# Attention and a gated long convolution on one core: from 2 by 384 to a 3 by 256 transform with woven products

## The chip, the core and the metric

The kernel runs on one core of a Trainium2 chip. A core has TensorE (PE in the profile), which multiplies matrices into PSUM; VectorE (DVE), ScalarE (ACT) and GpSimd (POOL), which work element by element; and SyncE (SP), which here only issues DMAs. The metric is device time in microseconds. Three runs of the kernel before took 190.65, 190.84 and 192.29 us; the median is 190.84.

## The reference

An attention over 4 batches, 8 heads, 768 positions and 64 channels per head. Heads with a flag see all earlier positions; the others see the first 4 positions and a window of the last 64. Its output, laid out as 4 x 768 x 512, goes through a gated convolution over the whole sequence:

```python
a = np.exp(scores - scores.max(-1, keepdims=True))      # scores masked per head
x = (a / a.sum(-1, keepdims=True)) @ v                  # 4 x 8 x 768 x 64, then to 4 x 768 x 512
proj = x @ w_proj
x1, x2, x3 = proj[..., :D], proj[..., D:2*D], proj[..., 2*D:]
X2 = np.fft.rfft(x2, n=S, axis=1)
H = np.fft.rfft(filter_fft, n=S, axis=0)
x2_conv = np.fft.irfft(X2 * H, n=S, axis=1)
out = (x1 * x2_conv * x3) @ w_out
```

D is 512 and S is 768. The transform is linear along the sequence, so it can be applied to x ahead of the product with the middle part of w_proj.

## The kernel before

The work is cut into named steps. The strings AHEAD and FAST list all steps in the order in which they are issued, with the PSUM bank they write (behind @) and the engine of those that can go to more than one (/v VectorE, /s ScalarE, /p GpSimd). Nothing is reordered later: each engine runs its steps in that order and waits on semaphores for what other engines make. A second, general kernel stands behind a branch for other flags; it isn't run here.

Heads are handled in 16 pairs, n = 0 to 15, four pairs to a batch b. Per pair: lk, lq, lv load k, q and v (SP issues them, L1369 and L1383); ck, cq, cv cast them; T and E bring q and k into the layout with channels on partitions, by TensorE and a copy for the first eight pairs, by a DMA transpose after that; sc are the products of scores (L1452), ex their exponentials on ScalarE (L1471); the mask is applied either by products that add a large negative bias (sb, L1465, for n below BIASED_FAST) or by multiplying the exponentials (mk and mr, L978); at are the products with v (L1516), rec and nm the normalization (L1533). A pair is all-causal (RR), all-windowed (LL) or mixed (RL); every four pairs have the same kinds in the same order.

Forward transform of a pair: fd and fe fold the two halves of the sequence into a difference and a sum of 384 rows; fA, fS, fb and fr combine their three blocks of 128; the half-transforms W (L1569, L1571, L1573; two per pair, each of three products of 256, 256 and 128 columns) give the spectrum of one chain in one PSUM bank each, written word after word; We evicts both. tn and te turn the normalized output (by TensorE for the pairs in TURNED_BACK, else by DMA) into xT.

Per batch b: X (L1620) multiplies the spectrum with the middle part of w_proj, in three tiles of two halves, four products of 512 columns each; Xe evicts; pa, pb, pc multiply with the filter's spectrum HAB (complex, on VectorE); sw are two DMAs that exchange the halves of a tile for pb. For each block cb of 128 channels: x1 and x3 (L1655) are the outer two projections; xs evicts x1; g multiplies x1 and x3. The inverse transform c (L1685) has two sums of three products of 384 columns, each sum in a bank of its own; ce copies one of them to SBUF as f_evs, and cv (L1696) adds and subtracts the other, which gives the two halves of the sequence; y multiplies with the gate. o (L1712) is the product with w_out, oe evicts, st stores.

Once at the start: iota, sine and cosine make the tables G of the forward transform; Gt (L1227) turns them on TensorE into the tables Gi of the inverse one. The filter is loaded by GpSimd's queue (lfilt, L1236), as are the weights (lw, lwo); F (L1265) transforms it with 18 products, H scales it into HAB, and Hd are two DMAs that exchange halves. blank (L1041) are 29 products of zeros, five in AHEAD and twelve pairs in FAST.

Of the kernel before, what the change touches and what calls it, by code (L numbers as in the profile page):

```python
# [9 lines left out]
FP32 = mybir.dt.float32  # L10
# [103 lines left out]
SIXTHS = (0, 1, 2, 3, 4, 5, 6, 7, 8, 9, 10, 11, 12, 13, 14, 15)  # L114
# [7 lines left out]
lflag lk0 lq0 lk1 lq1 mblank want tcol fcol0 table sin0 fcol1 blank0@6 tfrac quarter mtab0 par turns other angle  # L122
ident mtab1 wrap size sin cos
# [3 lines left out]
ones1 ones2 mtab3 blank5@0 lq2 lk2 blank10@1 ck0/v skew0/s lv0 parb skew1/p G32/s T0.1@2 xp0 cq0/v lk3 blank6@3  # L127
mtab2 E0.1/v lv1 blank8@4 Gk1/s lv3 blank7@5 Gm00 btab G31/p blank1@6 ck1/v kz1 lq3 T0.0@7 lk4 alt blank3@0 Gm2
cq1/s G30/p Gh0 lq4 T1.1@1 Gm01 kz0 lv2 E0.0/s G00/v T1.0@3 G01/p Gm1 cq2/s lk6 E1.1/v sc0.1@4 sb0.1 lq6 ck2/p
sc0.3@6 ex0.1 Gh1 E1.0/v sc0.4@0 ones0 kx1/p sb0.4 lk5 sb0.3 T2.1@2 ex0.4 kz2 lk7 sc0.0@4 E2.1/v lq5 cv0/p sb0.0  # L130
Gt1@3 ex0.3 lq7 blank2@0 kx2/v Gt2@1 Gk0/p ex0.0 lv6 T2.0@2 ks1/p Ge2/v ck3/p sc0.2@6 Ge1/s E2.0/v sc1.2@4 sb1.2
lfilt sb0.2 T3.1@0 ex1.2 sc0.5@2 Gt0@1 ex0.2 cv1/v sc2.3@4 E3.1/v lv4 vx1/p sb0.5 ex0.5 sc1.0@6 lw2.1 Ge0/v
sb1.0 ks2/s vs1/v at0.0@2 lw2.0 ex1.0 at0.1 cq3/v lw0.1 T3.0@0 ex2.3 kx3/v sc1.1@6 rec0 lw1.1 sb1.1 nm0/v cv3/s
blank11@1 ex1.1 sc2.1@4 fe0/p sb2.1 tn0@1 cq4/v E3.0/s at1.0@2 lw0.0 blank9@6 ex2.1 ks3/v sc2.4@6 ck4/v at1.1
lw1.0 ex2.4 T4.0@0 T4.1@4 vs3/v E4.0/s te0/v lwo sc3.1@6 sb3.1 rec1 E4.1/s nm1/v fd0/p sc3.2@0 sb3.2 ex3.1 fe1/v
tn1@5 fS0/p ex3.2 sc3.0@2 fold0/v sb3.0 sc2.0@6 ex3.0 vx3/v fd1/v F0.0@4 fA0/v fA1/p F0.1@0 H0.0/s fS1/v fb0/p
sb2.0 fold1/v sc2.2@2 H0.1/s sb2.2 ex2.0 fb1/p te1/v F1.0@1 fr1 ex2.2 F2.1@4 fr0 cv2/v H1.0/s F2.0 lv5 vs2/v
vx2/p H0.2/v at2.0@6 H2.0/s at2.1 ck6/p sc4.0@2 H2.1/s rec2 Hd0 at3.0@0 nm2/v at3.1 H2.2/s lk9 rec3 fe2/p F1.1@6
# [790 lines left out]
def patterned(tc, pools, pre, q, k, v, flags, n_sink, window, moe_w_proj, moe_filter_fft, moe_w_out, out):  # L929
# [912 lines left out]
```

## Time and profile before

| | |
|---|---|
| median of three runs | 190.84 us |
| profiled execution | 190.27 us |
| its span, first to last instruction | 188.4 us |
| granted TensorE clock, mean | 0.985 |
| DMA queue 1 (issued by SP): packets, MB, share of 16 engines | 75986, 30.81, 73.9% |
| DMA queue 0 (issued by GpSimd): packets, MB, share | 2944, 2.88, 9.1% |

Busy time is the time in which an engine had at least one instruction under way. Products overlap in TensorE's pipeline, so the mean duration of one is longer than its share of the time; the distance between the starts of neighbours, or a piece of the chain of waits divided by its count, is what one costs in a stream. The chain of waits follows the work that ended last back through whatever released each step. In rows of groups, the second number behind the bar is the mean duration of one instruction in ns, and what stands behind the second bar is idle time of the engine just ahead of it.

### The profile page before, as it was taken

What the parts mean: (1) busy time and instruction counts of PE and PEld (TensorE: products, weight loads), DVE (VectorE), ACT (ScalarE), POOL (GpSimd) and SP (SyncE); (2) the same over time, 40 slices, a digit from 0 to 9 for tenths busy, and PEclk for the clock granted to TensorE, in tenths of its full rate; (3) what the DMA queues carried; (4) which work ended last, traced back from release to release, by engine and by line L of the source; (5) the groups of instructions that cost most, each with busy time, mean ns of one, the idle gap of its engine ahead of it and who ended that gap; (6) DMA issues with size and microseconds to landing.
All of it is one profiled execution on the core that took longest, in us unless ns stands there. A gap on an engine that the chain in (4) does not pass through costs nothing.

```text
span 188.4 us, 4493 instructions
## 1 busy us (share of the span) xinstructions
PE 176.5 (94%) x1694; PEld 103.4 (55%) x1694; DVE 161.2 (86%) x329; ACT 145.6 (77%) x210; POOL 69.0 (37%) x103
## 2 busy tenths in 40 slices
PE   7879999989998999999999999999999999999970
PEld 2437664647745563575555656655657765555530
DVE  6887799789889999999989999999899996499810
ACT  5787899999999999988989999696977332426360
POOL 5874785554322224670250460700650630000000
PEclk9978999999999999999999999999999999999997
DMA  4999999999999999999999989982162002312074
GB/s 152 330 274 279 208 197 236 270 286 251 213 202 225 215 185 166 233 219 213 202 233 228 228 221 238 250 87 56 60 98 111 3 2 111 135 36 111 11 286 157
DMA packets 78955, 34.01 MB, mean 180 GB/s; under 512 B 68306, under 2 KB 75218, under 8 KB 78930
## 3 DMA queue, kind: packets, MB, share of 16 engines
q1 hardware_dynamic: 75986, 30.81, 73.9%
q0 software_dynamic: 2944, 2.88, 9.1%
q8 instruction: 14, 0.23, 0.5%
q14 instruction: 11, 0.09, 0.2%
HBM read 24.64 MB, written 6.29 MB: 164 GB/s over the span
## 4 chain that ended last, share of the span: by engine, by line
PE 66%; ACT 14%; DVE 6%; DMA 5%; issue 3%; POOL 2%; SPq 2%; DVEq 0%; ACTq 0%; POOLq 0%
PE space L1655 18%; PE space L1712 11%; PE space L1620 8%; PE space L1452 7%; PE space L1685 7%; PE space L1516 6%; ACT f_pT L1471 4%; DMA f_qkT<-f_qk_bf 3%; ACT f_HAB L1274 3%; DMA f_v_f<-in_v_dram 2%; PE space L1465 2%; ACT f_qk_bf L975 2%; SPq L1383 2%; PE space L1569 1%; PE space L1571 1%
## 5 line engine op out<-in xcount | busy, mean ns | idle before, releaser
L1471 ACT ACTIVATE f_pT<-space 128x1024 bf16<-128x1024 f32 (+3 forms) x68 | 58.8, 917 | 6.1 <-PE space L1465 1.9
L1655 PE MATMUL space<-f_xT,f_wproj 128*128 128x384 bf16 x256 | 47.9, 326 | 0.1
L1655 PEld LDWEIGHTS <-f_wproj 128*128 128x128 bf16 x256 | 24.0, 98 | 17.1 <-issue 1.0
L1712 PE MATMUL space<-f_wout,r_gy 128*128 128x512 bf16 x96 | 24.7, 379 | 0.0
L1452 PE MATMUL space<-f_qkT 64*128 64x128 bf16 (+3 forms) x248 | 22.6, 253 | 1.1 <-DVE f_attn L1533 0.5
L1620 PE MATMUL space<-f_wproj,f_xh 128*128 128x512 bf16 x96 | 22.7, 379 | 0.1
L1685 PE MATMUL space<-f_Gi,r_P 128*128 128x384 bf16 x96 | 19.0, 326 | 0.7 <-ACT f_evs L975 0.3
L978 DVE TENSOR_TENSOR f_pT<-f_pT,r_mtab 128x1024 bf16<-128x1024 bf16 (+3 forms) x33 | 18.5, 583 | 0.8 <-ACT f_pT L1471 0.6
L975 ACT COPY f_o<-space 128x1024 f32<-128x1024 f32 (+1 forms) x12 | 9.9, 836 | 11.3 <-PE space L1712 11.2
L1516 PEld LDWEIGHTS <-f_pT 128*128 128x128 bf16 x472 | 16.7, 97 | 3.6 <-issue 0.9
L1516 PE MATMUL space<-f_v_aug,f_pT 128*128 128x65 bf16 x392 | 17.9, 193 | 0.6 <-ACT f_X L975 0.5
L1452 PEld LDWEIGHTS <-f_qkT 64*128 64x128 bf16 x248 | 10.3, 94 | 13.1 <-issue 10.4
L978 POOL TENSOR_TENSOR f_uv<-f_fo 128x256 bf16<-128x256 bf16 x12 | 9.1, 766 | 21.1 <-DVE f_fo L978 15.8
L1696 DVE TENSOR_TENSOR f_conv<-f_evs,space 128x384 bf16<-128x384 f32 x32 | 16.1, 545 | 0.6 <-PE space L1685 0.3
L975 ACT CAST f_xh<-space 128x768 bf16<-128x768 f32 x14 | 11.2, 808 | 4.9 <-PE space L1573 4.6
L1620 PEld LDWEIGHTS <-f_xh 128*128 128x128 bf16 x96 | 9.0, 98 | 10.0 <-issue 0.4
L1712 PEld LDWEIGHTS <-r_gy 128*128 128x128 bf16 x96 | 9.0, 98 | 8.9 <-issue 0.4
L1533 DVE TENSOR_TENSOR f_attn<-space,f_rec 128x768 bf16<-128x768 f32 x14 | 13.4, 955 | 0.4
L1685 PEld LDWEIGHTS <-r_P 128*128 128x128 bf16 x96 | 8.8, 97 | 7.4 <-issue 1.1
L978 POOL TENSOR_TENSOR f_fo<-f_attn 128x384 bf16<-128x384 bf16 x11 | 10.4, 960 | 2.4 <-DVE f_attn L1533 1.9
L975 ACT CAST f_X<-space 128x1024 bf16<-128x1024 f32 x8 | 8.2, 1020 | 2.8 <-PE space L1620 2.7
L978 POOL TENSOR_TENSOR f_pT<-f_pT,r_mtab 128x512 bf16<-128x512 bf16 (+1 forms) x6 | 6.8, 1146 | 9.1 <-ACT f_pT L1471 9.1
(136 smaller groups left out, 345.7 us busy)
## 6 DMA issues: line engine op xcount, KB each, us to landing
f_v_f<-in_v_dram SPq DMA_DIRECT2D x32, 192.0 KB, 4.7
out_dram<-f_o SPq DMA_DIRECT2D x9, 512.0 KB, 3.1
r_qk_f<-in_k_dram SPq DMA_DIRECT2D x10, 192.0 KB, 4.4
r_qk_f<-in_q_dram SPq DMA_DIRECT2D x10, 192.0 KB, 5.0
r_qk_f<-in_k_dram SPq DMA_DIRECT2D x4, 384.0 KB, 11.3
r_qk_f<-in_q_dram SPq DMA_DIRECT2D x4, 384.0 KB, 6.1
f_qk_f<-in_q_dram SPq DMA_DIRECT2D x4, 384.0 KB, 5.8
f_qk_f<-in_k_dram SPq DMA_DIRECT2D x4, 384.0 KB, 6.6
```

Source lines behind the costliest of these rows:

```text
L975: nc.scalar.copy(out=out, in_=in_)
L978: (nc.gpsimd if now["engine"] == "p" else nc.vector).tensor_tensor(out, a, b, op)
L1274: nc.scalar.activation(out=out_(), in_=in_(), func=AF.Copy, scale=w / S)
L1452: nc.tensor.matmul(sc[:, bank, col:col + 128 * cnt], lhsT=keys, rhs=qkT(n)[rows, 0, 128 * i:128 * (i + cnt)], start=(col == 0 or not biase ...
L1471: nc.scalar.activation(out=pT(n)[:, c, :, 0:w], in_=held[f"sc.{n}.{c}"][:, :, 0:w], func=AF.Exp, scale=SCALE)
L1516: nc.tensor.matmul(att[:, hh, 65 * i:65 * i + 65], lhsT=pT(n)[:, c, bank, col:col + 128], rhs=values, start=(z == 0), stop=(z == len(here) ...
L1533: nc.vector.tensor_mul(attn(n).rearrange("p i hh d -> p hh i d"), rows[:, :, :, 0:64], held[f"rec.{n}"][:, :, :, None].to_broadcast([128, ...
L1620: nc.tensor.matmul(ps[:, u, :], lhsT=xh(b)[:, cc, chain, 128 * part:128 * part + 128], rhs=wproj()[:, cc, DM:2 * DM], start=(cc == 0), sto ...
L1655: nc.tensor.matmul(ps[:, s, 0:HS], lhsT=wproj()[:, cc, part * DM + cb * 128:part * DM + (cb + 1) * 128], rhs=xT(b)[:, cc, s * HS:s * HS + HS],
L1685: nc.tensor.matmul(ps[:, 0, 0:HS], lhsT=P(b)[:, t, u, ch], rhs=Gi()[:, tile_no], start=(m == 0), stop=(m == 2))
L1696: fn(conv[:, half * HS:half * HS + HS], held[f"evs.{b}.{cb}"], held[f"c_ps.{b}.{cb}.1"][:, 0, 0:HS])
L1712: nc.tensor.matmul(ps, lhsT=gy(b)[:, cb, i * 128:(i + 1) * 128], rhs=wout()[:, cb, :], start=(cb == 0), stop=(cb == NC - 1))
```

## The change

The order 2 by 384 becomes the prime-factor order 3 by 256. What is computed stays the same; the steps between change, and with them the whole order string.

- The two half-transforms of a pair write into the same bank, one the even and the other the odd words, 512 words in the first bank and 256 in the second (`woven`); the eviction then reads 768 words in a row. Products and columns stay as they were.
- The filter goes the same way: folds, the same four combinations (fAF, fSF, fbF, frF), eight half-transforms K, an eviction Ke, 24 transposes F, and scalings H. The 18 products and the exchanging DMAs go.
- The tables of the inverse transform come straight from sine and cosine; the 18 transposes go.
- A three-point step of nine operations per batch (qa, qs, qr, qh, qz, qd, qb, qp, qm) stands between the spectrum's product and the inverse. The DMA exchanges sw go; pb reads X itself.
- The inverse has six products of 256 columns per block of channels, in sums of two, for the three classes of positions modulo 3. ce and the two cv per block go. In batches 0 to 2, y reads the result straight from PSUM; in batch 3, one cv on ScalarE copies 768 columns to SBUF first.
- Positions in gy are sorted by class, so g and xs read PSUM with a step of three words, and stores write rows that lie three apart.
- BIASED_FAST goes from 4 to 8: pairs 4 to 7 get bias products, and their mk and mr steps go. Pair 14 leaves TURNED_BACK. A one-element GpSimd copy, gate, that reads the loaded k of pair 3 stands ahead of lfilt.
- The order string is new throughout. In batch 3, x1 and x3 products stand between the spectrum and the inverse, and all o2 products ahead of the spectrum. The same 29 blank products remain; nine of the twelve pairs in FAST stand ahead of the first scores (seven before).

```diff
-TURNED_BACK = (0, 1, 2, 3, 4, 5, 6, 7, 14, 15)
-BIASED_FAST = 4
+TURNED_BACK = (0, 1, 2, 3, 4, 5, 6, 7, 15)
+BIASED_FAST = 8
+DIRECT = ((0, 0), (0, 1), (0, 2), (0, 3), (1, 0), (1, 1), (1, 2), (1, 3), (2, 0), (2, 1), (2, 2), (2, 3))
...
+    @op("gate")
+    def _():
+        nc.gpsimd.tensor_copy(out=buf("gate", [1, 1], FP32), in_=held["qk_f32.3"][0:1, 0, 0, 0, 0:1])
...
+    def spectrum(ps, u, uv, br, ch):
+        woven = lambda bank, count: ps[:, bank, 0:2 * count].rearrange("p (f u) -> p u f", u=2)[:, u]
+        nc.tensor.matmul(woven(0, 256), lhsT=br[:, 1, u, ch], rhs=G()[:, 3 * u:3 * u + 2], start=True, stop=False)
+        nc.tensor.matmul(woven(0, 256), lhsT=uv[:, 2 * u, ch], rhs=Gk()[:, u], start=False, stop=True)
+        nc.tensor.matmul(woven(1, 128), lhsT=br[:, 0, u, ch], rhs=G()[:, 3 * u + 2], start=True, stop=True)
+
+    def taken(x, ps):
+        ev(x.rearrange("p g f -> p (g f)"), ps.rearrange("p a f -> p (a f)")[:, 0:S])
...
-                ps = banks(f"W_ps.{n}")
-                if n in SIXTHS:
-                    nc.tensor.matmul(ps[:, u, 0:256], lhsT=br(n)[:, 1, u], rhs=G()[:, 3 * u:3 * u + 2, 0],
-                                     start=True, stop=False)
-                    nc.tensor.matmul(ps[:, u, 0:256], lhsT=uv(n)[:, 1 + 2 * u], rhs=Gk()[:, u],
-                                     start=False, stop=True)
-                    nc.tensor.matmul(ps[:, u, 256:384], lhsT=br(n)[:, 0, u], rhs=G()[:, 3 * u + 2, 0],
-                                     start=True, stop=True)
...
+                spectrum(banks(f"W_ps.{n}"), u, uv(n), br(n), slice(0, 128))
...
-            ev(xh(b)[:, hp], held[f"W_ps.{n}"][:, :, 0:HS])
+            taken(xh(b)[:, hp], held[f"W_ps.{n}"])
...
+    def classes(ps):
+        return ps[:, :, 0:HS].rearrange("p h (t s) -> p s h t", s=3)
...
+        @op(f"qa{b}")
+            two(SD(b)[:, 0:2], P(b)[:, 1], P(b)[:, 2], ALU.add)
+        @op(f"qs{b}")
+            two(SD(b)[:, 2:4], P(b)[:, 1], P(b)[:, 2], ALU.subtract)
+        @op(f"qr{b}")
+            scale(SD(b)[0:1], flat(b)[0:1, 2:6], 2.0)
+        @op(f"qh{b}")
+            scale(Y0(b), P(b)[:, 0], 0.5)
+        @op(f"qz{b}")
+            two(Y0(b), Y0(b), SD(b)[:, 0:4:3], ALU.add)
+        @op(f"qd{b}")
+            scale(SD(b)[:, 1:3], SD(b)[:, 1:3], 2.0 * KAPPA)
+        @op(f"qb{b}")
+            two(P(b)[:, 0], P(b)[:, 0], SD(b)[:, 0:4:3], ALU.subtract)
+        @op(f"qp{b}")
+            two(flat(b)[:, 2:4], P(b)[:, 0], SD(b)[:, 1:3], ALU.add)
+        @op(f"qm{b}")
+            two(flat(b)[:, 4:6], P(b)[:, 0], SD(b)[:, 1:3], ALU.subtract)
...
-            for r in range(2):
-                @op(f"c{b}.{cb}.{r}")
-                    ps = banks(f"c_ps.{b}.{cb}.{r}", count=1)
-                    for m, (t, u, tile_no) in enumerate(INVERSE[r]):
-                        nc.tensor.matmul(ps[:, 0, 0:HS], lhsT=P(b)[:, t, u, ch], rhs=Gi()[:, tile_no],
-                                         start=(m == 0), stop=(m == 2))
...
+            @op(f"c{b}.{cb}")
+                ps = banks(f"c_ps.{b}.{cb}").rearrange("p a f -> p (a f)")
+                for s, (re, im) in enumerate(POINTS):
+                    for c, rows in enumerate((re, im)):
+                        rhs = Gi()[:, c].rearrange("p a f -> p (a f)")[:, START[s]:START[s] + 256] if s else Gj()[:, c]
+                        nc.tensor.matmul(ps[:, 256 * s:256 * s + 256], lhsT=rows(b)[:, ch], rhs=rhs,
+                                         start=(c == 0), stop=(c == 1))
+
+            if (b, cb) not in DIRECT:
+                @op(f"cv{b}.{cb}")
+                    ev(buf(f"conv.{b}.{cb}", [128, S], BF16, f"conv{cb % 2}"),
+                       held[f"c_ps.{b}.{cb}"].rearrange("p a f -> p (a f)")[:, 0:S])
...
+                if (b, cb) in DIRECT:
+                    to = y if cb < NC - 1 else buf(f"conv.{b}.{cb}", [128, S], BF16, f"conv{cb % 2}")
+                    nc.vector.tensor_mul(to, held[f"c_ps.{b}.{cb}"].rearrange("p a f -> p (a f)")[:, 0:S], x)
...
+                    rows = out[b].rearrange("(n p s) c -> s p n c", p=128, s=3)[i // 2]
```

The order of batch 3 after the change, from its first spectrum product to its inverse:

```
X3.2.0@0 st2.1 X3.2.1 X3.1.0@4 Xe3.2/s X3.1.1 pb3.2/v X3.0.0@2 pa3.2/v Xe3.1/s x13.0.0@0
pc3.2/v oe2.5/s pb3.1/v X3.0.1 pa3.1/v st2.5 x13.0.1 Xe3.0/s pc3.1/v x13.3.0@4 xs3.0/s pa3.0/v x13.2.0@6 qa3/v
x13.3.1 pb3.0/v x33.0.0@2 xs3.3/s qs3/v x13.1.0@0 pc3.0/v qr3/s x33.0.1 qh3/v x13.1.1 g3.0 x33.1.1@4 qd3/s qb3/v
x33.1.0 qz3/v x13.2.1 xs3.1/s qp3/v x33.2.1@2 xs3.2/s qm3/v x33.2.0 g3.1 c3.0@0 g3.2 c3.1@6 cv3.0/s c3.2@4
```

More of the change, by code (lines that the diff above doesn't have):

```diff
@@ L1252, in _ @@
     def _():
-        two(fold()[:, 0], filt()[:, 0:NM, :], filt()[:, NM:NT, :], ALU.subtract)
+        two(fold()[:, 0], filt()[:, 0:NM, :], filt()[:, NM:NT, :], ALU.add)
     @op("fold1")
     def _():
-        two(fold()[:, 1], filt()[:, 0:NM, :], filt()[:, NM:NT, :], ALU.add)
-    for t, pieces in enumerate((((0, 0), (0, 1)), ((1, 3), (1, 4)), ((0, 2), (1, None)))):
-        for u, (chain, tile_no) in enumerate(pieces):
-            @op(f"F{t}.{u}")
-            def _(t=t, u=u, chain=chain, tile_no=tile_no):
-                ps = banks("F_ps2")[:, u] if t == 2 else banks(f"F_ps{t}.{u}", count=1)[:, 0]
-                for m in range(NM):
-                    nc.tensor.matmul(ps, lhsT=Gh()[:, m] if tile_no is None else G()[:, tile_no, m, :],
-                                     rhs=fold()[:, chain, m, :], start=(m == 0), stop=(m == NM - 1))
```

428 lines of the change are left out of this document (205 added, 223 removed).

## The prediction

> **What bounds the kernel now.** I read the busy shares first, then busy time by stage, then the chain of waits, then groups by form. The first fence is from the page: the span, the busy shares, and the chain's shares by engine. The second is busy time in five stretches (columns: stretch, its length, then busy us and instruction count of PE, weight loads, VectorE, ScalarE, GpSimd; granted clock; DMA share; GB/s).
>
> ```profile
> span 188.4 us, 4493 instructions
> PE 176.5 (94%) x1694; PEld 103.4 (55%) x1694; DVE 161.2 (86%) x329; ACT 145.6 (77%) x210; POOL 69.0 (37%) x103
> ...
> PE 66%; ACT 14%; DVE 6%; DMA 5%; issue 3%; POOL 2%; SPq 2%; DVEq 0%; ACTq 0%; POOLq 0%
> ```
>
> ```profile
> 0.00:40.00 40.00, 35.95 (x396) 20.72 (x397) 32.80 (x73) 34.17 (x46) 25.99 (x53) 0.96 1.07 245
> 40.00:80.00 40.00, 37.79 (x404) 22.94 (x403) 37.24 (x78) 39.31 (x57) 15.09 (x19) 1.00 1.10 217
> 80.00:120.00 40.00, 40.00 (x400) 23.52 (x399) 38.08 (x83) 36.16 (x54) 15.13 (x20) 1.00 1.17 227
> 120.00:160.00 40.00, 40.00 (x379) 24.67 (x378) 36.59 (x73) 25.40 (x41) 12.76 (x14) 1.00 0.37 75
> 160.00:188.40 28.40, 22.73 (x121) 11.51 (x118) 16.46 (x27) 10.60 (x15) 0.00 (x0) 0.96 0.34 122
> ```
>
> Two regimes show. Up to 80 us ScalarE is fullest (39.31 of 40 us from 40 to 80) and TensorE is idle for 4.05 + 2.21 = 6.3 us. From 80 to 160 us TensorE has no idle time at all, and VectorE is close behind with 38.08 + 36.59 = 74.7 of 80 us. So what TensorE no longer does after 80 us comes off the span, as long as VectorE can follow; before 80 us extra TensorE work is partly free. The chain of waits (start, us, what) shows the end:
>
> ```profile
> 166.29 0.65 PE space L1655 x4
> ...
> 171.11 2.44 PE space L1685 x15
> ...
> 177.55 5.19 PE space L1712 x24
> ...
> 182.77 0.59 ACT f_o L975
> ```
>
> From 166.29 to 182.74 us it is products alone, then a copy (L975) and the last store. I take the price of a product from its share of the chain or from the distance between starts, since the mean of a row holds the pipeline's depth too: 2.44/15 = 0.163 us for 384 columns (L1685), 0.65/4 = 0.163 again (L1655), 5.19/24 = 0.216 for 512 (L1712).
>
> **The inverse transform.** A block of 128 channels now takes six products of 256 columns, not six of 384. The price of 256 columns comes from the forward transform in the timeline of TensorE (start, us, line):
>
> ```profile
> 39.84 0.27 PE L1569 MATMUL space<-r_G,f_br 128*128 128x256 bf16 x1 [0.25 <-ACT f_pT L1471]
> 39.95 0.27 PE L1571 MATMUL space<-f_Gk,f_uv 128*128 128x256 bf16 x1
> 40.05 0.22 PE L1573 MATMUL space<-r_G,f_br 128*128 128x128 bf16 x1
> 40.11 0.27 PE L1569 MATMUL space<-r_G,f_br 128*128 128x256 bf16 x1
> ```
>
> Starts lie 0.11 and 0.10 apart, and a half of the transform (256, 256 and 128 columns) takes 40.11 - 39.84 = 0.27; with 0.055 for 128 columns that is 0.107 for 256. Sixteen blocks: 96 x 0.163 = 15.6 becomes 96 x 0.107 = 10.3, so -5.3 us, nearly all of it after 80 us.
>
> **Setup, filter, transposes.** Pieces of the chain price these:
>
> ```profile
> 18.09 0.44 PE space L1227 x6
> ...
> 29.66 0.77 PE space L1265 x3
> ...
> 148.10 0.33 PE space L1589 x6
> ```
>
> The 18 transposes of the inverse tables (L1227) go: about -1.3 at 0.44 per six. The filter's 18 products (L1265, 512 columns) cost 18 x 0.216 = 3.9; in their place come eight halves at 0.27 and 24 transposes at 0.055 (six take 0.33, L1589), 3.5 in all: -0.4. Pair 14 goes back by DMA, not by transposes: -0.3, after 80 us. The blank products stay 29; of their twelve pairs nine now stand ahead of the first scores, seven before. There TensorE waits for loads and table work in either order, so the move costs 0; without that cover two pairs cost 4 x 0.216 = 0.9, within the 6.3 us of idle time of that stage.
>
> **Masks of pairs 4 to 7** become bias products, as pairs 0 to 3 have them. Pairs 0 to 3 have the same kinds, so their 33 products are the price (three forms, counts behind x):
>
> ```profile
> L1465 PE MATMUL space<-f_btab,r_identity 128*128 128x512 bf16 x10 | 3.2, 384 | 0.0
> L1465 PE MATMUL space<-f_btab,r_identity 128*128 128x128 bf16 x18 | 2.7, 249 | 0.0
> L1465 PE MATMUL space<-f_btab,r_identity 128*128 128x384 bf16 x5 | 1.3, 332 | 0.0
> ```
>
> At the spacing above that is 10 x 0.216 + 5 x 0.163 + 18 x 0.057 = 4.0 us more for TensorE. Together with setup and filter it makes 4.0 - 1.3 - 0.4 = +2.3 before 80 us. There ScalarE ends most waits and TensorE has 6.3 us idle, so it costs between 0 and 2.3; I take 1.0.
>
> **VectorE.** Rows by form (line, operation, shapes, count | busy, mean ns):
>
> ```profile
> L1696 DVE TENSOR_TENSOR f_conv<-f_evs,space 128x384 bf16<-128x384 f32 x32 | 16.1, 545 | 0.6 <-PE space L1685 0.3
> L978 DVE TENSOR_TENSOR r_P<-r_P,f_m 128x1024 bf16<-128x1024 bf16 x12 | 8.2, 687 | 0.1
> L978 DVE TENSOR_TENSOR f_pT<-f_pT,r_mtab 128x1024 bf16<-128x1024 bf16 x12 | 8.1, 697 | 0.0
> L971 DVE COPY f_qkT<-space 128x768 bf16<-128x768 bf16 x8 | 7.6, 950 | 0.9 <-PE space L1407 0.9
> L1674 DVE TENSOR_TENSOR r_gy<-r_x1s,space 128x768 bf16<-128x768 bf16 x8 | 7.5, 942 | 0.3 <-PE space L1655 0.3
> L975 ACT COPY f_evs<-space 128x384 f32<-128x384 f32 x14 | 6.8, 493 | 3.1 <-DVE f_conv L1696 2.2 <-PE space L1685 0.8
> L978 DVE TENSOR_TENSOR r_gy<-f_conv,r_gy 128x768 bf16<-128x768 bf16 x10 | 5.7, 569 | 0.1
> L978 DVE TENSOR_TENSOR f_pT<-f_pT,r_mtab 128x512 bf16<-128x512 bf16 x10 | 5.2, 525 | 0.2
> L978 DVE TENSOR_TENSOR f_pT<-f_pT,r_mtab 128x768 bf16<-128x768 bf16 x9 | 4.9, 549 | 0.6 <-ACT f_pT L1471 0.6
> L1129 DVE TENSOR_SCALAR f_btab<-r_mtab 128x896 bf16<-128x896 bf16 x1 | 0.4, 395 | 0.4 <-POOL r_mtab L1113 0.4
> ```
>
> Off: 32 sums of the two halves (L1696), 32 x 0.545 = 17.4; the y products, 13 x 0.569 = 7.4; masks of pairs 4 to 7, at least 4 x 0.697 + 3 x 0.549 + 3 x 0.525 = 6.0. On: y read straight from PSUM in 12 blocks, priced by the PSUM product of equal size (L1674), 12 x 0.942 = 11.3, and four at 0.569 = 2.3; 23 sums of 1024 elements per partition for the three-point step (its 24th is on GpSimd), 23 x 0.687 = 15.8; four scalings at some 0.45 (L1129 takes 0.395 for 896) = 1.8; the filter's three combinations, 2.1. Net: 33.3 - 30.8 = +2.5, and without the masks and the filter, which fall before 80 us, +6.4. Against that, three evictions of x1, one normalization and the setup's tables leave VectorE (four of 768 elements at 0.95, as L971: 3.8 of it after 80 us). So after 80 us it has 0 to 6, say 2.6, more to do in 5.6 us less: 38.08 + 36.59 + 16.46 = 91.1 of the 102.7 us up to 182.74 (89%) become 93.7 of 97.1 (96%). What TensorE then waits costs between 0 and 5.6 (the whole gain); I take 0.6, near the lower end, as from 80 to 160 us products run without a gap beside a VectorE that is 93% full.
>
> Reading x1 and x3 from PSUM with a step of three words I cost at nothing: the eviction of qkT (L971, 950 ns) reads words far apart and takes what L1674 takes with neighbours; on ScalarE both take 802 ns:
>
> ```profile
> L975 ACT CAST f_X<-space 128x1024 bf16<-128x1024 f32 x8 | 8.2, 1020 | 2.8 <-PE space L1620 2.7
> L975 ACT COPY f_qkT<-space 128x768 bf16<-128x768 bf16 x8 | 6.2, 802 | 0.1
> L975 ACT CAST f_x1s<-space 128x768 bf16<-128x768 f32 x7 | 5.5, 802 | 0.8 <-PE space L1655 0.8
> ```
>
> ScalarE loses 14 copies at 0.493 (L975, f_evs) = 6.9 and gains four conv evictions at 0.8 and scalings at about 1.02 (f_X, 1024 elements), half of them in batch 3, where it has room: 10.6 of 28.4 us. That is free except in the tail.
>
> **The tail of batch 3.** After its last spectrum product TensorE has 13 groups of x1 and x3 at 0.65 in front of the inverse: 8.5 us. Beside them VectorE runs, after an eviction of 1.02 on ScalarE, pa, qa, pb, qs at 0.69 each (to 3.8) and pc, qh and a gate product (to 5.9). The difference qs also opens the one-row scaling on ScalarE (2048 elements, at most twice 1.02, to 5.9) and qd after it (to 6.9). Then qb, qz, qp and qm at 0.69 end at 8.6. The inverse can start at 8.6, so TensorE is idle for 0.1 to 0.2 us. A shorter row scaling makes that 0, queues that slip make it 2; I take 0.2.
>
> **DMA and queues.** Ten exchanges by SP go (eight swaps of X, two of the filter); nothing on the chain waited for them, 0. One wait is added: GpSimd's copy (gate) holds back lfilt, the six weight loads and lwo until the key load of pair 3 has landed:
>
> ```profile
> L1236 POOL DMA_DIRECT2D r_gy<-in_moe_filter_fft_dram x1: 1062/1062/1062, 14.9 to 14.9; - x1
> f_qk_f<-in_k_dram SPq DMA_DIRECT2D x4, 384.0 KB, 6.6
> out_dram<-f_o SPq DMA_DIRECT2D x6, 256.0 KB, 3.3
> ```
>
> Behind it wait GpSimd's v_x and mask copies, and the filter's fold on VectorE. The filter load is issued at 14.9 us now; the load it waits for is the fourth k load that SP issues, and such loads take 6.6 to land, so I take the wait to be open by then: 0, and with that cover gone a few us of a stage where TensorE has 6.3 idle. Stores go to rows three apart; a row is still one partition's 2 KB, so I leave the last store at 3.3.
>
> **Products into every second word.** The forward transform now writes the even or odd words of a bank. No row of this trace shows such a write. A gain is excluded: the same columns stream. From above the row of 512 columns bounds it, since a woven product of 256 passes over the same 512 words: 0.216 in place of 0.107, and 0.11 for 128 columns, so 0.27 more for each half. I take 0 for the forecast: the products quoted here, 128 to 512 columns, are priced by their columns alone, whatever they read. [...]
>
> **Sum.** 188.4 - 5.3 - 0.3 + 1.0 + 0.2 + 0.6 = 184.6 us of span. Around the span lie 190.27 - 188.4 = 1.9, so 186.5 against the profiled run, and that run is 0.6 under the median of 190.84: **187.1 us**, 2% faster. Its own range is 185.3 (nothing paid for masks, tail and waiting) to 190.5 (masks 1.3 more, tail 1.8, waiting 0.3).
>
> **Rivals.** *Woven writes are slow (slower).* Its place is the 32 halves of the forward transform and the filter's eight; its price is up to 0.27 each, 10.8 us. Pairs 6 to 15, 20 halves, stand behind the scores of pair 8 in the new order, so after 80 us, and pay 5.4 in full; the other 20 pay between 0 and 5.4, say 2.7: 187.1 + 8.1 = 195.2 (192.5 to 197.9). It decides from 3.7/8.1, 46% of the full price, when a half takes 0.39 in place of 0.27. For it: every transform sits in a stretch of back-to-back products. Against: it has no row. *VectorE becomes the bound.* The three-point step queues nine operations between spectrum and inverse; TensorE stands while it waits. If all 5.6 us go back in place of the 0.6, it is 192.1; if half do, 189.3; between them 190.7. For it: 96% full by my own ledger. Against: the new order puts other products between the two. That the inverse does not get cheaper is hardly a case: its columns fall by a third.
>
> **Chances.** Forecast 0.50, woven writes 0.33, VectorE 0.17. A measurement of this kernel tells about 1% from no change. The forecast lies under 188.9 in 0.85 of its cases; VectorE's case falls mostly within 1%; woven writes are nearly always over 192.7. Faster 0.42 + 0.02 = 0.44, within 1% 0.07 + 0.13 + 0.01 = 0.21, slower 0.01 + 0.02 + 0.32 = 0.35. The range 185.3 to 195.2 holds the forecast, VectorE's case and the lower half of the woven one, about 0.8.
>
> **What would show it.** Right: inverse products start 0.107 apart, halves of the forward transform 0.27 apart, TensorE idle under 2 us from 80 us to the last spectrum of batch 3, no gap over 0.5 us ahead of batch 3's inverse. Wrong: woven products 0.2 apart (first rival); TensorE waiting for VectorE's sums for over 3 us after 80 us (second); the inverse's gap at 3 us or more (tail mis-sized); TensorE waiting for the filter or the weights before 50 us (gate).

## The result: 5% slower, and where it was lost

| | before | after |
|---|---|---|
| median of the runs, us | 190.75 (190.39 to 192.29) | 200.44 (200.10 to 202.08) |
| ratio, 95% interval | | 1.051 (1.043 to 1.059) |
| profiled execution, us / its span, us | 190.27 / 188.4 | 200.56 / 198.7 |

The forecast was 187.1, its range 185.3 to 195.2: wrong in sign and outside the range. The page of the changed kernel, span and busy shares:

```profile
span 198.7 us, 4521 instructions
PE 183.2 (92%) x1714; PEld 111.3 (56%) x1733; DVE 155.6 (78%) x304; ACT 154.2 (78%) x226; POOL 74.7 (38%) x109
```

Its busy time by stage (columns as before):

```profile
0.00:40.00 40.00, 33.17 (x364) 20.12 (x368) 28.06 (x64) 36.03 (x61) 26.04 (x52) 0.96 1.07 255
40.00:80.00 40.00, 39.64 (x399) 24.75 (x399) 30.21 (x55) 29.41 (x39) 20.30 (x28) 1.00 1.22 216
80.00:120.00 40.00, 38.41 (x395) 23.28 (x398) 37.12 (x76) 37.55 (x58) 11.88 (x15) 1.00 0.92 188
120.00:160.00 40.00, 39.19 (x378) 24.61 (x384) 38.00 (x74) 30.91 (x46) 13.89 (x13) 1.00 0.24 65
160.00:198.70 38.70, 32.79 (x187) 18.52 (x188) 22.22 (x37) 20.33 (x25) 2.59 (x3) 0.98 0.29 102
```

TensorE should have had less to do; its busy time rose from 176.5 to 183.2 us (with 1714 products beside 1733 weight loads, 19 records of products are missing). VectorE's fell by 5.6 and ScalarE's rose by 8.6. Where TensorE's time went is plain from its groups by form (count | busy us, mean ns):

```profile
L1271 PE MATMUL space<-f_Gk,f_uv 128*128 128x256 bf16 x32 | 13.6, 424 | 0.0
L1270 PE MATMUL space<-r_G,f_br 128*128 128x256 bf16 x32 | 13.0, 405 | 0.0
L1272 PE MATMUL space<-r_G,f_br 128*128 128x128 bf16 x32 | 10.0, 314 | 0.0
L1711 PE MATMUL space<-f_Gi,r_P 128*128 128x256 bf16 x64 | 9.8, 272 | 0.0
```

Lines 1270 to 1272 are the forward transform, which writes every second word; line 1711 is the inverse, which writes neighbouring words. Both stream 256 columns: 405 to 424 ns against 272. The mean holds the pipeline's depth, so the price is read from the distance of starts, at a granted clock of 1.00 (timeline of TensorE):

```profile
166.26 0.42 PE L1270 MATMUL space<-r_G,f_br 128*128 128x256 bf16 x1
166.48 0.42 PE L1271 MATMUL space<-f_Gk,f_uv 128*128 128x256 bf16 x1
166.69 0.31 PE L1272 MATMUL space<-r_G,f_br 128*128 128x128 bf16 x1
166.80 0.42 PE L1737 MATMUL space<-f_wout,r_gy 128*128 128x512 bf16 x1
```

Starts lie 0.22, 0.21 and 0.11 apart: one half-transform takes 166.80 - 166.26 = 0.54 us, where it took 0.27. That is the full price of the first rival, the upper bound to the digit. A second thing shows at the front, in the chain of waits (start, us, what):

```profile
21.07 10.68 DMA r_qk_f<-in_q_dram
```

The q load of pair 7 is on the chain for 10.68 us: ScalarE's copy of it stands ahead of exponentials that TensorE waits for.

### The profile page after: what moved, and what is told of

Same layout as the page of the kernel before. It is cut to its first block, busy times and chain, and to the rows that moved or that the text cites. A ratio compares the mean times of both kernels' runs of the same rounds, so it can differ in the third digit from the quotient of the medians.

```text
span 198.7 us, 4521 instructions
## 1 busy us (share of the span) xinstructions
PE 183.2 (92%) x1714; PEld 111.3 (56%) x1733; DVE 155.6 (78%) x304; ACT 154.2 (78%) x226; POOL 74.7 (38%) x109
## 4 chain that ended last, share of the span: by engine, by line
PE 72%; ACT 13%; DMA 5%; DVE 3%; issue 3%; DVEq 0%
PE space L1684 20%; PE space L1619 10%; PE space L1737 10%; PE space L1465 7%; PE space L1529 6%; DMA r_qk_f<-in_q_dram 5%; PE space L1270 5%; PE space L1271 4%; ACT f_pT L1484 4%; PE space L1711 3%; PE space L1478 3%; PE space L1272 2%; ACT f_qk_bf L973 1%; ACT f_conv L973 1%; ACT f_qkT L973 1%
## 5 line engine op out<-in xcount | busy, mean ns | idle before, releaser
L1684 PE MATMUL space<-f_xT,f_wproj 128*128 128x384 bf16 x256 | 46.3, 327 | 0.5 <-DVE f_attn L1546 0.3
L1737 PE MATMUL space<-f_wout,r_gy 128*128 128x512 bf16 x89 | 23.3, 381 | 0.7 <-ACT f_xh L973 0.3
L1529 PEld LDWEIGHTS <-f_pT 128*128 128x128 bf16 x472 | 18.0, 101 | 4.0 <-issue 1.0
L973 ACT COPY f_o<-space 128x1024 f32<-128x1024 f32 (+1 forms) x13 | 11.5, 887 | 7.9 <-PE space L1737 7.9
L971 POOL COPY f_v_x<-f_v_aug 64x520 bf16<-64x520 bf16 (+1 forms) x12 | 6.7, 558 | 27.7 <-ACT f_v_aug L973 17.2
L1737 PEld LDWEIGHTS <-r_gy 128*128 128x128 bf16 x96 | 8.9, 100 | 9.5 <-DVE r_gy L1703 1.0
L976 DVE TENSOR_TENSOR f_pT<-f_pT,r_mtab 128x512 bf16<-128x512 bf16 (+3 forms) x23 | 13.4, 588 | 1.0 <-ACT f_pT L1484 0.8
L1271 PE MATMUL space<-f_Gk,f_uv 128*128 128x256 bf16 x32 | 13.6, 424 | 0.0
L976 POOL TENSOR_TENSOR f_uv<-f_fo 128x256 bf16<-128x256 bf16 x10 | 6.8, 683 | 16.7 <-DVE f_fo L976 10.6
L1270 PE MATMUL space<-r_G,f_br 128*128 128x256 bf16 x32 | 13.0, 405 | 0.0
L1478 PE MATMUL space<-f_btab,r_identity 128*128 128x128 bf16 (+2 forms) x63 | 12.2, 288 | 0.4 <-issue 0.3
```

The costliest lines, as they stand in the source:

```text
L973: nc.scalar.copy(out=out, in_=in_)
L976: (nc.gpsimd if now["engine"] == "p" else nc.vector).tensor_tensor(out, a, b, op)
L1270: nc.tensor.matmul(woven(0, 256), lhsT=br[:, 1, u, ch], rhs=G()[:, 3 * u:3 * u + 2], start=True, stop=False)
L1271: nc.tensor.matmul(woven(0, 256), lhsT=uv[:, 2 * u, ch], rhs=Gk()[:, u], start=False, stop=True)
L1478: nc.tensor.matmul(held[f"sc.{n}.{c}"][:, bank, 128 * at:128 * (at + width)], lhsT=identity(), rhs=btab()[:, what:what + width], start=Fal ...
L1529: nc.tensor.matmul(att[:, hh, 65 * i:65 * i + 65], lhsT=pT(n)[:, c, bank, col:col + 128], rhs=values, start=(z == 0), stop=(z == len(here) ...
```

## The experiments

Each time stands beside the kernel before on the same chip (medians 190.1 to 190.8). Runs on different chips are compared by their ratios.

### The weaving, taken out and put in alone

e1: the change, with each half in a bank of its own, in neighbouring words; the copy out of PSUM weaves.

```
-        woven = lambda bank, count: ps[:, bank, 0:2 * count].rearrange("p (f u) -> p u f", u=2)[:, u]
-        nc.tensor.matmul(woven(0, 256), lhsT=br[:, 1, u, ch], ...
+        nc.tensor.matmul(ps[:, u, 0:256], lhsT=br[:, 1, u, ch], ...
...
+        ev(x.rearrange("p (f u) -> p f u", u=2), ps[:, :, 0:HS].rearrange("p u f -> p f u"))
```

> The changed kernel with one thing undone: each half-transform writes 384 neighbouring words in a bank of its own, and the eviction weaves them by reading PSUM with a step of a bank. Theory A (woven products run at half rate and this is the loss): halves of the forward transform start 0.27 us apart again, not 0.54; 40 halves give back 8.1 to 10.8 us of the 200.4, so 189.6 to 192.3 us. Rival B (the new order and the waits for VectorE's nine operations cost it, and the slow woven products mostly hide): 196 us or more. If the forecast of the other terms was right as well, it would be 187.1 us.

Measured: 192.22, ratio 1.008 (1.005 to 1.010). Its halves start 106.13 - 105.86 = 0.27 us apart again (timeline of TensorE):

```profile
105.86 0.27 PE L1269 MATMUL space<-r_G,f_br 128*128 128x256 bf16 x1
106.13 0.27 PE L1269 MATMUL space<-r_G,f_br 128*128 128x256 bf16 x1
```

e2 is the kernel before with the weaving and nothing else (its copy out of PSUM reads with a step of two):

```
-                    nc.tensor.matmul(ps[:, u, 0:256], lhsT=br(n)[:, 1, u], ...
+                    nc.tensor.matmul(woven(0, 256), lhsT=br(n)[:, 1, u], ...
...
```

> The kernel before with weaving alone: the products of the forward transform write every second word, the eviction reads with a step of two; order and all else as before. Theory A: each of 32 halves takes 0.54 us in place of 0.27; those after 80 us (some 20) pay in full, 5.4 us, the rest between 0 and 3.2, so 196 to 199.5 us. Rival B: under 193 us.

Measured: 198.03, ratio 1.040 (1.037 to 1.043). So the weaving costs 200.44 - 192.22 = 8.2 us in the change and 198.03 - 190.55 = 7.5 alone: the main cause, shown from both sides. What is left of the change is 192.22 - 190.55 = 1.7 us slower than before, not 3.7 faster.

### What a strided write is paid by

e3: the change, woven by aligned pairs of words (two of one half, two of the other).

```
-        woven = lambda bank, count: ps[:, bank, 0:2 * count].rearrange("p (f u) -> p u f", u=2)[:, u]
+        woven = lambda bank, count: ps[:, bank, 0:2 * count].rearrange("p (f u j) -> p u f j", u=2, j=2)[:, u]
...
```

> The changed kernel with the products woven by pairs of words (two written, two left out) in place of single words; the eviction sorts them. The same 512 words are passed over and the pattern is still not contiguous. Line theory (a product pays for each pair of neighbouring words that it opens): as fast as without weaving, 189.6 to 192.3 us, halves at 0.27 us. Span theory (it pays for every word that it passes over) and gap theory (any gap halves the rate): no change, 199 to 201 us, halves at 0.54 us.

Measured: 192.61, ratio 1.007 (1.005 to 1.010), as without weaving, though it passes over the same 512 words and leaves as many of them out. m1 adds eleven series of twelve products behind the last one of the kernel before: 256 columns contiguous, at step 2 and at step 2 from the odd word; 128 at steps 1, 2, 3, 4; by pairs, by pairs from an odd word (254), by fours; 255 contiguous from an odd word.

```
...
+    series("s256x2", 256, lambda ps: ps[:, 0:512].rearrange("p (f u) -> p u f", u=2)[:, 0])
...
+    series("s128x4", 128, lambda ps: ps[:, 0:512].rearrange("p (f u) -> p u f", u=4)[:, 0])
...
+    series("s254pairodd", 254, lambda ps: ps[:, 1:509].rearrange("p (f u j) -> p u f j", u=2, j=2)[:, 0])
...
```

> The kernel before with eleven series of twelve products appended behind its last product; only the distance between starts within a series counts. Line theory: 256 columns 0.107 us in a row, 0.215 at step 2 from an even or an odd word; 128 columns 0.055 at step 1, 0.107 at steps 2, 3 and 4 alike; 256 by aligned pairs or fours 0.107, 254 by pairs that start at an odd word 0.21; 255 in a row from an odd word 0.107. Span theory: 128 columns 0.107 at step 2, 0.16 at step 3, 0.215 at step 4; pairs and fours 0.215. Gap theory: every pattern with gaps at twice the price of its columns, 0.107 for all of 128 and 0.215 for all of 256.

Its groups by form:

```profile
L1744 PE MATMUL space<-r_X 128*128 128x256 bf16 x60 | 9.7, 333 | 0.0
L1744 PE MATMUL space<-r_X 128*128 128x128 bf16 x48 | 4.8, 290 | 0.0
L1744 PE MATMUL space<-r_X 128*128 128x254 bf16 x12 | 2.7, 416 | 0.0
L1744 PE MATMUL space<-r_X 128*128 128x255 bf16 x12 | 1.5, 272 | 0.0
```

and, in its timeline, the one row that holds all eleven series (start, us):

```profile
182.88 17.75 PE L1744 MATMUL space<-r_X 128*128 128x256 bf16 x132
```

The first two rows by form mix several series. Narrow windows of the timeline hold one series each; these four show 256 columns at step 2, 128 at step 4, 256 by aligned pairs and 256 by aligned fours:

```profile
184.58 1.07 PE L1744 MATMUL space<-r_X 128*128 128x256 bf16 x4
192.84 0.86 PE L1744 MATMUL space<-r_X 128*128 128x128 bf16 x6
194.08 0.71 PE L1744 MATMUL space<-r_X 128*128 128x256 bf16 x5
197.96 0.71 PE L1744 MATMUL space<-r_X 128*128 128x256 bf16 x5
```

A row lasts from its first start to its last end, so the duration of one product comes off (0.42, 0.31, 0.28 and 0.28 us, the means of these windows). Starts then lie (1.07 - 0.42)/3 = 0.217 apart at step 2, (0.86 - 0.31)/5 = 0.11 for 128 columns at step 4, and (0.71 - 0.28)/4 = 0.11 by pairs and by fours. For 128 columns the windows at steps 2 and 3 have the same 0.86 us for six. Pairs that begin at an odd word, so that each lies across two aligned ones, take 416 ns, as if woven; 255 contiguous words from an odd one take 272, as if aligned. In these series the price thus goes by how many aligned pairs of fp32 words a product touches, about 0.84 ns each: 0.215 us for 256 pairs (in the change, (166.69 - 166.26)/2), 0.107 where two columns share one. Summed so, the eleven series take 17.4 us; by words passed over it would be 21.9; the timeline has 17.75 with the last product's depth. Aligned pairs and fours leave words out as well and start 0.11 us apart, like neighbouring words in the kernel before (0.107), so a gap by itself was not paid for in these series.

### The front: exponentials, loads, clock

In e1 TensorE waits at the front as in the change; the longest wait of each row (TensorE's waits: who waits, for whom, us, times, longest) lies between 29 and 34 us:

```profile
PE space L1464 <- ACT f_pT L1483: 2.6, 3, 2.1
PE space L1419 <- ACT f_qk_bf L973: 2.3, 3, 1.3
```

and from 34 us it runs at a low granted clock (busy time from 26 to 34 and 34 to 40 us; the clock stands behind the five engines):

```profile
26.00:34.00 8.00, 4.28 (x55) 2.60 (x54) 5.99 (x14) 6.92 (x10) 1.45 (x2) 0.91 1.15 267
34.00:40.00 6.00, 6.00 (x78) 5.11 (x76) 4.49 (x7) 5.93 (x10) 4.42 (x3) 0.56 1.18 243
```

e5 puts two exponentials ahead of these copies, e6 gives the first normalization to VectorE, e8 delays three weight loads, e10 fills the gap with blank products ("..." marks steps left out):

```
e5  -ex2.4 fS1/v ck6/s sb2.0 ... fr0 cq7/s fold1/v ex2.0 lq10 vs3/p ex3.1
    +ex2.4 sb2.0 ex2.0 ex3.1 fS1/v ck6/s ... ex3.2 cq7/s lq10
e6  -nm0/s +nm0/v
e8  -lwo ... lw1.0 ... lw1.1 (21 to 25 us)   +fA2/p lw1.0 lw1.1 lwo ex4.3 (about 45 us)
e10 +blank13@3 T6.1@2 ... blank14@3 T6.0@3   (5 and 9 products)
```

> The unwoven kernel (192.2 us) with the exponentials of pairs 2 and 3 (ex2.0, ex3.1) ahead of the copies of pair 6 on ScalarE and with the copy of pair 7's q, which waits for its load until 32 us, behind ex3.2. Theory F (ScalarE stands in that copy while exponentials that TensorE waits for are ready): TensorE's 2.1 us of waiting at 31.8 to 33.9 us falls to under 0.7, and the time to 189.5 to 191.2. Rival V (VectorE paces the middle, so what is won at the front is lost again from 108 to 150 us): the wait falls, but the time stays within 191.7 to 192.5. Rival D (loads are what everything waits for up to 40 us): TensorE's idle time from 26 to 40 us stays at 3.5 to 3.9 us, and the time with it.

> The unwoven kernel (192.2 us) with the first normalization (nm0: 12 pieces, 2.6 us on ScalarE at 22.4 us) back on VectorE, where the kernel before has it. If ScalarE's queue ahead of 30 us is what makes TensorE late: 190.5 to 191.7, and TensorE's idle time from 22 to 34 us falls from 4.3 us by 1 or more. If loads set that stretch (ScalarE waits 0.96 us for a load at 29.6 in any case): within 191.8 to 192.5.

> The unwoven kernel (192.2 us) with three of the weight loads (the output weights and the two of the spectrum's products, 1.0 MB, issued on GpSimd at 21 to 25 us, first needed after 55 us) issued at about 45 us. At the 265 GB/s that the DMA engines move from 26 to 34 us that is 3.9 us of transfers out of the way of the loads of pairs 6 and 7. Theory D (these loads hold TensorE from 26 to 34 us): the load of pair 7's q lands at 29 us or before in place of 32.0, TensorE's idle time from 26 to 40 us falls from 3.7 us to under 2, and the time is 189.0 to 190.8. Rival (the loads queue on SP's own, or other work sets the stretch): landing within 0.7 us of 32.0 and time within 191.7 to 192.6.

> The unwoven kernel (192.2 us) with 14 more blank products of 512 columns on TensorE where it waits: five ahead of the first transpose of pair 6, nine behind it (29 to 33 us). In the unwoven kernel the products that follow that gap run at half the pace: the transform's 256 columns start 0.21 us apart at 36.9 to 39.3 us and 0.11 apart from 39.4 on, at a granted clock of 0.56 from 34 to 40 us. Theory C (the gap itself costs about 2.7 us more by the slower clock behind it): granted clock 0.9 or more from 34 to 40 us, 0.11 apart throughout, and 189.3 to 191.0. Rival (loads and ScalarE set the pace up to 45 us whatever the clock): the clock is up and the time within 191.7 to 192.6. If the blank products are themselves in the way: above 192.6.

| run | time, us | ratio to before (95%) |
|---|---|---|
| e1 unwoven | 192.22 | 1.008 (1.005 to 1.010) |
| e5 exponentials first | 192.94 | 1.014 (1.007 to 1.021) |
| e6 first normalization on VectorE | 192.12 | 1.009 (1.006 to 1.013) |
| e8 late weights | 191.36 | 1.004 (1.000 to 1.008) |
| e10 blank products in the gap | 192.45 | 1.014 (1.005 to 1.022) |

e5 took the wait for the exponentials away and found others: TensorE then waits 2.4 us for copies of q and k and 1.8 for a combination on VectorE. e6 is no different. e8 is 0.8 us better, with an interval that overlaps e1's. e10 raised the clock, as it was built to, and gained nothing (26 to 34 and 34 to 40 us):

```profile
26.00:34.00 8.00, 7.34 (x72) 4.10 (x70) 6.29 (x14) 7.30 (x10) 1.44 (x2) 1.00 1.15 268
34.00:40.00 6.00, 4.34 (x78) 3.45 (x77) 4.80 (x8) 5.93 (x10) 4.65 (x3) 1.00 1.18 243
```

The clock is 1.00 in place of 0.56, and TensorE's busy time there falls from 6.00 to 4.34: it waits more. ScalarE is busy 5.93 of 6 us in both, and the DMA engines move 243 GB/s in both. So the slow clock by itself did not cost the time there. That ScalarE and the loads set that stretch fits these rows but isn't shown. None of the four runs did away with the waiting: between 26 and 40 us TensorE is idle for 3.7 us in e1 (1.0 in the kernel before), 4.9 in e5, 2.8 in e6 and in e8, and in e10 blank products stand in the gap. With the same 0.9 us less of it than e1, e6 was no faster and e8 gained 0.8. What the front costs in all therefore stays open.

### The masks

e7 leaves the new bias products out, e9 puts the masks back on VectorE:

```
e7  -                    for bank in range(2):
    +                    for bank in range(2 if n < 4 else 0):
    ...
e9  -BIASED_FAST = 8
    +BIASED_FAST = 4
    -... sb4.1 ... sb7.0      +... mk4.0/v ... mk7.0/v mr6/v
```

> The unwoven kernel (192.2 us) with the bias products of pairs 4 to 7 left out, so that these four pairs are not masked: 33 products, 4.0 us of TensorE less. It gives the price of the masks as products, which the forecast took as 1.0 (0 to 2.3 together with setup and filter, 4.0 by itself). If TensorE is on the path where they stand (from 28 to 80 us it is full in the unwoven kernel but for 3.6 us): 188.7 to 190.5. If ScalarE or VectorE paces that stretch or takes it back later: 191.5 to 192.3.

> The unwoven kernel (192.2 us) with the masks of pairs 4 to 7 undone: products on VectorE after the exponential, as in the kernel before, and no bias products for these four pairs. TensorE does 4.0 us less, VectorE 7 to 8 us more. With the bias products simply left out it took 190.6, which is the floor here. If VectorE has room from 40 to 80 us (it is 72 to 97% full there): 190.4 to 191.2. If it hands the work back: 191.5 to 192.5, and the bias products cost nothing net.

Measured: e7 190.58, ratio 1.000 (0.997 to 1.003); e9 194.37, ratio 1.021 (1.014 to 1.028). The 4.0 us of products cost 1.5 of the time (0.8% of 190.6), but having the masks on VectorE costs 2.5 more than that way (1.3%), at the places in the order that this run gave them. From 40 to 80 us e9 has

```profile
40.00:80.00 40.00, 33.45 (x374) 21.48 (x372) 37.52 (x71) 30.80 (x41) 22.11 (x27) 0.98 1.12 212
```

VectorE at 37.52 of 40 us, and TensorE idle for 6.5. In this order the masks' move, by itself, is a gain.

### Who sets the pace from 80 to 160 us

TensorE, VectorE and ScalarE all look full there in e1:

```profile
80.00:120.00 40.00, 39.01 (x410) 23.57 (x412) 38.32 (x83) 39.37 (x62) 13.45 (x16) 1.00 1.17 210
120.00:160.00 40.00, 39.06 (x374) 24.66 (x380) 37.66 (x70) 27.71 (x43) 14.81 (x14) 1.00 0.24 74
```

The following runs take work from one engine at a time.

```
sums out (e4 on e1; e12, e14, e15 on e8):   +            if b == 3:   (ahead of qz, qb, qp, qm)
products out (e13, e15 on e8; e16 on before):
-                        for cc in range(NC):
+                        for cc in range(3 if b in (1, 2) else NC):
norms (e11, e12 on e8):  -nm0/s nm7/s nm12/s   +nm0/v nm7/v nm12/v
```

> The unwoven kernel (192.2 us) with four of the three-point sums of VectorE (qz, qb, qp, qm) left out in batches 0, 1 and 2: 12 operations of about 0.69 us, 8.3 us of VectorE less (154.9 to about 146.6), all between about 80 and 150 us. Theory V (VectorE paces TensorE from about 108 to 150 us): 188.6 to 190.3, 2 to 3.5 us less, and the chain of waits from 108 to 150 us turns from VectorE to products. Rival F (all that is left was lost ahead of 50 us, and VectorE only looks late): 191.7 to 192.3, no change over 0.5.

> The unwoven kernel with the late weight loads (191.4 us), with the normalizations of pairs 0, 7 and 12 as one product of 0.96 us each on VectorE in place of 12 pieces, 2.6 us in all, on ScalarE. Theory S (ScalarE, 98% full from 80 to 120 us, sets the pace there): 189.8 to 190.9. Theory V (VectorE sets it): 191.5 to 192.6, slower by up to the 1.9 us that VectorE gets. Theory P (TensorE itself is the bound after 80 us): within 191.1 to 191.7.

> The kernel of the run before (norms on VectorE) with the twelve three-point sums qz, qb, qp, qm of batches 0 to 2 left out as well: 7.8 us less on ScalarE and 5.4 less on VectorE than the unwoven kernel with late weights. If ScalarE and VectorE take turns in setting the pace (each relieved alone gave 0.7 us at most): 187.6 to 189.6, and TensorE has no idle time from 80 to 160 us. Theory P: 190.6 to 191.4.

> The unwoven kernel with the late weight loads (191.4 us), with one of the four products left out of each accumulation of x1 and x3 in batches 1 and 2: 32 products of 384 columns, 5.2 us of TensorE less, all between 80 and 150 us. Theory P (TensorE is the bound there): 186.2 to 187.6. If ScalarE and VectorE set the pace: 189.9 to 191.3, and TensorE's busy time falls while the gaps grow.

> The unwoven kernel with the late weight loads (191.4 us), with the twelve three-point sums of batches 0 to 2 left out (VectorE 8.3 us less). Alone, on the early weight loads, this gave 0.7. Joint theory (TensorE and VectorE bind at nearly the same level from 80 to 160 us, each less than 1.5 us behind the other): 190.2 to 191.0. If VectorE alone were the bound: under 189.

> The same with the 32 products of x1 and x3 in batches 1 and 2 left out as well (TensorE 5.2 us less). The products alone gave nothing (191.5), the sums alone are the run before. Joint theory: the two together give far more than the sum of the two, 186.5 to 189.0. If ScalarE (98% full from 80 to 120 us) or the loads are the real bound: 189.8 or more.

> The kernel before (190.6 us) with one of the four products left out of each accumulation of x1 and x3 in batches 1 and 2: 32 products of 384 columns, 5.2 us of TensorE less between 80 and 160 us, nothing else touched. The forecast's premise (TensorE has no idle time from 80 to 160 us, so what it no longer does there comes off the span): 185.0 to 186.5. Joint limits already in the kernel before (VectorE 93% full, ScalarE and the loads behind it): 188.0 to 190.0.

| run | taken or moved (count times price), us | time, us | ratio to before (95%) |
|---|---|---|---|
| e4 | VectorE -8.3, on e1 | 191.47 | 1.007 (1.004 to 1.010) |
| e8 | the reference of the next five | 191.36 | 1.004 (1.000 to 1.008) |
| e11 | ScalarE -7.8, VectorE +2.9 | 193.41 | 1.016 (1.008 to 1.024) |
| e12 | ScalarE -7.8, VectorE -5.4 | 191.99 | 1.008 (1.004 to 1.012) |
| e13 | TensorE -5.2 | 191.46 | 1.006 (1.001 to 1.010) |
| e14 | VectorE -8.3 | 191.46 | 1.006 (1.003 to 1.009) |
| e15 | TensorE -5.2, VectorE -8.3 | 189.84 | 0.997 (0.993 to 1.001) |
| e16 | TensorE -5.2, on the kernel before | 188.82 | 0.990 (0.986 to 0.994) |

Less for TensorE alone: nothing (e13). Less for VectorE alone: nothing that can be told (e4, e14). Both together: 0.7% less than e8, 0.9% less than either alone (e15); its interval touches those of e8 and e13 at the end. More for VectorE, in exchange for much less on ScalarE: 1.2% more (e11, its interval too overlaps e8's a little). Less for ScalarE and VectorE together: nothing, against an expected 187.6 to 189.6 (e12). The whole busy time of VectorE fell by less than the sums taken from it, by 4.7 us in e14 and 7.2 in e15; why is not shown. In e13 the gaps simply open; 80 to 120 and 120 to 160 us:

```profile
80.00:120.00 40.00, 36.90 (x379) 21.85 (x378) 37.35 (x85) 39.05 (x61) 13.44 (x16) 1.00 1.20 210
120.00:160.00 40.00, 38.58 (x368) 23.60 (x367) 36.19 (x66) 28.07 (x44) 15.02 (x14) 1.00 0.26 82
```

The joint theory looks right in that the two taken together do more than the sum of the two, and was wrong in size: it had 186.5 to 189.0 for e15 and the time is 189.84. What is late next stands in e15's chain of waits: a k load, a transposition by DMA, exponentials.

```profile
76.46 3.18 DMA f_qk_f<-in_k_dram
79.64 0.75 ACT f_pT L1483
80.39 6.18 DMA f_qkT<-f_qk_bf
...
90.29 1.84 ACT f_pT L1483 x2
```

TensorE and VectorE thus seem to lie within about 1% of each other. That loads and ScalarE come next is read from this chain alone: no run takes work from TensorE and ScalarE together. e16 shows that TensorE wasn't the only limit in the kernel before either: 5.2 us of products less took 1.9 off the time (1.0% of 190.8), 37%. No run beat the kernel before with its whole computation in place.

## Why the prediction was wrong

**Woven writes at 0.** This is the step that failed: "I take 0 for the forecast: the products quoted here, 128 to 512 columns, are priced by their columns alone, whatever they read." Those rows held no strided write, so they said nothing on it; the argument "the same columns stream" bounds the price from below only. The forecast's own upper bound, 0.27 us for each half, was the measured price (0.54 - 0.27), and its first rival's 8.1 us was the cost (8.2). A quarter of the full 40 x 0.27 = 10.8 was hidden. The rival held in place and price, at a chance of 0.33 where no row spoke against it. The bound's reason, words passed over, did not hold: woven by aligned pairs, the change passes over the same 512 words and takes 192.61 us (e3), next to the 192.22 without weaving.

**What TensorE no longer does comes off the span.** This step was too strong, with its term "What TensorE then waits [...] I take 0.6". Its reason was that products run without a gap beside a VectorE that is 93% full. e16 tests that in the kernel before: 37% came off the time. Carried over to the 5.6 us saved after 80 us (5.3 + 0.3), some 2.1 would reach the end, and the term would be 3.5; that is an estimate, since e16's products came from other places than the inverse's. e1's own rows speak for less (the first two stages; the next two stand above):

```profile
0.00:40.00 40.00, 32.37 (x362) 20.18 (x367) 28.05 (x64) 35.88 (x61) 25.93 (x52) 0.91 1.06 255
40.00:80.00 40.00, 39.10 (x437) 25.00 (x437) 33.74 (x64) 33.07 (x44) 21.18 (x28) 1.00 1.07 208
```

TensorE's idle time from 80 to 160 us went from nothing to 0.99 + 0.94 = 1.9 us (1.1 in e8, whose trace lacks no product), and in its list of waits from 80 to 158 us only 0.8 us are for VectorE. In the first 40 us it went from 4.05 to 7.63, and from 40 to 80 us it fell from 2.21 to 0.90. By these readings the term was 1.1 to 3.5 in place of 0.6, and its size stays open. Most of the added idle time is at the front, where the forecast put the moved blank products and the gate at 0 and had no other term. The time of the unwoven change, 192.22, is next to the second rival's 189.3 to 192.1, but that rival's sign, over 3 us of waiting for VectorE after 80 us, isn't there.

VectorE's load itself was forecast well: 93.7 us after 80 us, and 93.1 in e1. ScalarE's was not: the forecast had it lose 6.9 us and gain four copies and some scalings, off the path but for the tail, and did not enter there the three copies of x1 and the normalization that it took off VectorE (their rows by form grew from 9.6 to 12.2 us and from 5.1 to 7.8 in the change). ScalarE went from 145.6 to 153.2 us in e1, and from 80 to 120 us from 36.16 to 39.37 of 40. That fits e13, which gained nothing, but no run shows that ScalarE is why.

**The sum.** 187.1 + 8.2 (weaving) + 0.5 to 2.9 (1.1 to 3.5 in place of 0.6) = 195.8 to 198.2. The other 2.2 to 4.6 us of the 200.4 are not explained. The early weight loads may hold 0.8 of them (e8); the rest of the front is a place to look, not a shown cause.

**Masks, setup and filter at +1.0.** Sized about right: the forecast charged 1.0 of 2.3 us of products (43%), and e7 gives 1.5 of 4.0 (38%). What it left out is that VectorE's relief ahead of 80 us has a worth of its own (e9).

**Confirmed.** The inverse's price: six products of 256 columns take 0.67 us in the chain of waits of the changed kernel, 0.11 each.

```profile
183.66 0.67 PE space L1711 x6
```

The gate, in GpSimd's timeline: its copy runs at once, with no idle time ahead of it, and the filter's load follows.

```profile
19.06 0.40 POOL L1223 COPY f_gate<-f_qk_f 1x1 f32<-1x1 f32 x1
19.41 1.06 POOL L1227 DMA_DIRECT2D r_gy<-in_moe_filter_fft_dram  x1
```

The load was issued 4.5 us later than before; TensorE did not wait for the filter or the weights, and VectorE 0.2 us for the filter. The tail: no wait is listed in front of batch 3's inverse; the one row of TensorE's waits after 158 us is 0.2, ahead of an output product (L1737). The forecast had 0.1 to 0.2 ahead of the inverse.

```profile
PE space L1737 <- DVE r_gy L1703: 0.2, 1, 0.2
```

**Not seen.** The stall ahead of 34 us, 2.0 us behind ScalarE and 1.4 behind copies of pair 6. The forecast looked there for the gate and the weights, not for a copy that waits for its load in front of exponentials in a queue that runs in order. The four runs on the front gained 0.8 us at most, but none of them removed the idle time, so they do not show that it is worth little.

## What to carry to other kernels

Here 256 columns cost 0.107 us written in a row and 0.215 written to every second word, so the price from the rows did not hold for a pattern that they did not show. Where an edit makes a pattern that no row has, measure it by itself first, or forecast from the upper bound. Let the copy out of PSUM do the weaving, or weave by aligned pairs of words: neither showed a price here (e1's copy takes 803 ns beside 808 before; e3 is at a ratio of 1.007, e1 at 1.008). Where an engine is full and its neighbours are at 90% and more, do not count on the whole of what is taken from it: here 37% came off in one kernel (e16, 1.9 of 5.2 us) and nothing in another (e13, 191.46 beside 191.36). And look at what the change hands to the neighbours.

## What the runs showed of the hardware

- In m1 (granted clock 1.00) a product's write to PSUM was paid by aligned pairs of fp32 words touched: 0.107 us for 256 columns in pairs or fours, 0.217 at step 2; 128 columns cost the same 0.11 at steps 2, 3 and 4.
- ScalarE's copy out of PSUM showed no such price: the copy of e1 that reads two banks alternately takes 803 ns (e1, groups by form),

```profile
L973 ACT CAST f_xh<-space 128x768 bf16<-128x768 f32 x14 | 11.2, 803 | 0.5 <-PE space L1271 0.5
```

and the one of the kernel before, which reads neighbours, 808:

```profile
L975 ACT CAST f_xh<-space 128x768 bf16<-128x768 f32 x14 | 11.2, 808 | 4.9 <-PE space L1573 4.6
```

- After the waits at the front TensorE ran for some 5 us at half pace and then at full (e1, timeline; starts 0.21 apart up to 39.27 us, 0.11 from 39.47; granted clock 0.56 from 34 to 40 us). With blank products in the waits (e10) the granted clock was 1.00 there, and the end did not move: 192.45 us beside 192.22.

```profile
39.06 0.41 PE L1269 MATMUL space<-r_G,f_br 128*128 128x256 bf16 x1
39.27 0.31 PE L1270 MATMUL space<-f_Gk,f_uv 128*128 128x256 bf16 x1
...
39.47 0.27 PE L1269 MATMUL space<-r_G,f_br 128*128 128x256 bf16 x1
39.58 0.27 PE L1270 MATMUL space<-f_Gk,f_uv 128*128 128x256 bf16 x1
```
